# Block sums copied by transfer instead of VectorE, and expert 0's second weight loaded in two halves

## The chip, the cores and the metric

One core of a Trainium2 chip. The metric is the device time of one execution in microseconds (us), taken over several executions; "span" is the part of it that the trace covers, from the first to the last recorded instruction. A second number of each run is the mean granted TensorE clock over the span (1.000 is full speed all the time). All runs here count as fast runs: on a single core no other core tells a disturbed run apart. The engines are TensorE (PE in the profile), VectorE (DVE), ScalarE (ACT), POOL, which here also issues the loads, and SP, which here issues transfers and nothing else. A "hole" is a stretch in which TensorE stands idle.

## The reference, cut to what matters

Attention over batch 4, 8 heads, 768 positions of width 64. Each query sees the keys within 16 positions and 24 summaries, one for each block of 32 positions (maximum of the keys, mean of the values). The result is fed to a mixture of 8 experts, each of two matrices (512x1024 and 1024x512), with routing weights balanced by eight normalising rounds.

```python
k_sum = k.reshape(B, H, nb, block, D).max(axis=3)      # block = 32
v_sum = v.reshape(B, H, nb, block, D).mean(axis=3)
# ... near scores within 16 positions and block scores, one softmax over both ...
v_all = np.concatenate([v, v_sum], axis=2)
out_attention = np.matmul(a, v_all)
# ...
for e in range(E):
    h = np.maximum(x @ w1[e], 0.0)
    out += P[:, e:e + 1] * (h @ w2[e])
```

## The kernel before

The 32 (batch, head) combinations are worked as 16 pairs, which the text numbers 0 to 15. The attention stage takes about the first 115 us; expert 0 is threaded into it, and experts 1 to 7 follow. The first matmuls with expert 0's second weight (w2) are called the first projection. In pairs 4 to 15 (`i >= PB`) the last matmul of the values stage multiplies one 128-row matrix `V_e` (`NE` = 2 buffers) for each chunk of 128 positions: rows 0 to 63 hold the block sums of the two heads (`vs` on TensorE; written by `block_out` on VectorE, the same for all six chunks), rows 64 to 127 the values just outside the chunk ("near values"; the four small transfers that bring them, on SP for i < 12 (`BY_DMA`), are the near copies).

```python
def block_sums(i):                       # TensorE, into a PSUM bank of the ring "a"
    ...
def block_out(i):                        # VectorE: scales the sums, frees that bank
    vs = at.pop(("vs", i))[0:64, :].rearrange("p (j d) -> p j d", j=2)
    dst = V_s[i][0:64, :] if i < PB else V_e[i % NE][0:64, 0, :]
    nc.vector.tensor_tensor(out=dst..., in0=vs, in1=own_n..., op=ALU.mult)
    if i >= PB:                          # PB = 4; the same sums for chunks 1 to 5
        ve = V_e[i % NE]                 # NE = 2 buffers
        nc.vector.tensor_copy(out=ve[0:64, 1:G, :],
                              in_=ve[0:64, 0:1, :].to_broadcast([64, G - 1, 2 * VD]))

def near_values(i):                      # four small transfers, on SP for i < 12
    ...
def key_max(i):                          # VectorE, needs the transposed keys kT
    nc.vector.tensor_reduce(out=ks[r][:, 0, 0:24], in_=kT[r]..., op=ALU.max)

def scores(i):                           # TensorE
    sg = at["sg", i, 0] = banks2("sg")
    if i >= WHOLE:                       # WHOLE = 12: the second half of the scores
        dst[1] = [bank("a", "sg1") for _ in range(2)]    # takes two banks of ring "a"
    ...
```

No order of instructions is written down by hand. The kernel holds a list scheduler ("the planner"): each piece of work is a unit with an engine, an estimated cost, dependencies, a priority and a `lag`, the delay until others can use its result. The planner simulates the engines and so fixes each engine's program order; on the chip every engine then works through its own list. The keys and queries of pairs 12 to 15 are transposed by a transfer (units `kT`); the planner gives it 1.7 us plus a lag of 2.0.

```python
U["vs", i] = add("PE", 0.4, lambda: block_sums(i), [U["v", i], U.get(("A", i - NE, 1)), ...], opens=[buf])
U["Vs", i] = add("DVE", 0.28 if i < PB else 0.7, lambda: block_out(i), [U["vs", i], sc], uses=[buf])
U["near", i] = add("SP" if i < BY_DMA else "POOL", 2.4 ..., lag=5.0 ...)
U["kT", i, z] = add("DMA", 1.7, None, [U["tr", i, z]], prio, lag=2.0)
# ...
load_pair(PB, "kqv")                     # pair 4's keys, queries, values
load("w2", lambda: load_w2(0), 0.85, 4.0)   # 1 MB
```

The softmax here doesn't subtract the row's maximum and nothing guards it: scores larger than these inputs give would overflow.

Of the kernel before, what the change touches and what calls it, by code (L numbers as in the profile page):

```python
# [10 lines left out]
BF16 = mybir.dt.bfloat16  # L11
F16 = mybir.dt.float16
# [116 lines left out]
def kernel(  # L129
# [64 lines left out]
    def load_w2(e):  # L194
        w2s[e] = wpool.tile([128, KF, DM], F16, tag="w2", name="w2")
        nc.gpsimd.dma_start(out=w2s[e][:], in_=moe_w2[e].rearrange("(fk p) d -> p fk d", p=128))
# [21 lines left out]
    NQ = 6  # L218
    NB = PB
    NE = 2  # L220
    NS = 1
    NA = 3
    stage = ExitStack()
    with tc.manual_schedule():
# [22 lines left out]
        V_e = [attn.tile([128, G, 2 * VD], BF16, name=f"Ve{i}") for i in range(NE)]  # L247
# [110 lines left out]
        def block_out(i):  # L358
            vs = at.pop(("vs", i))[0:64, :].rearrange("p (j d) -> p j d", j=2)
            dst = V_s[i][0:64, :] if i < PB else V_e[i % NE][0:64, 0, :]  # L360
            nc.vector.tensor_tensor(out=dst.rearrange("p (j x) -> p j x", j=2)[:, :, 0:D], in0=vs,
                                    in1=own_n[:].to_broadcast([64, 2, D]), op=ALU.mult)
            if i >= PB:
                ve = V_e[i % NE]
                nc.vector.tensor_copy(out=ve[0:64, 1:G, :],
                                      in_=ve[0:64, 0:1, :].to_broadcast([64, G - 1, 2 * VD]))


        def near_values(i):

            sv, ve = v_x[i % NQ], V_e[i % NE]
            eng = nc.sync if i < BY_DMA else nc.gpsimd
            for j in range(2):
                c0, q0 = VD * j, 64 + 32 * j
                eng.dma_start(out=ve[q0 + W:q0 + 2 * W, 1:G, c0:c0 + VD],
                              in_=sv[128 - W:128, j, 0:G - 1, :])
                eng.dma_start(out=ve[q0:q0 + W, 0:G - 1, c0:c0 + VD],
                              in_=sv[0:W, j, 1:G, :])
# [48 lines left out]
        def values(i, h):  # L427
            sv, ee, ve, em = v_x[i % NQ], E_e[i % NE], V_e[i % NE], at["em", i]
            av = at["av", i, h] = bank("a", "av")
            for cc in range(HG):  # L430
                c, o = HG * h + cc, cc * 2 * VD
                for j in range(2):
                    nc.tensor.matmul(av[:, o + j * VD:o + (j + 1) * VD],  # L433
                                     lhsT=em[:, j, c, :], rhs=sv[:, j, c, :],
                                     start=(cc == 0 and j == 0), stop=False,
                                     skip_group_check=True)
            for cc in range(HG):
                c, o = HG * h + cc, cc * 2 * VD
                nc.tensor.matmul(av[:, o:o + 2 * VD], lhsT=ee[:, c, :], rhs=ve[:, c, :],  # L439
                                 start=False, stop=True, skip_group_check=True)  # L440
# [419 lines left out]
        def load(key, fn, issue, us, deps=()):  # L860
            last[0] = add("POOL", issue, fn, [last[0], *deps])
            last[1] = add("DMA", us, None, [add("RING", 0, None, [last[0]], lag=1.4 if last[1] else 0.9), last[1]], 100.0)
            U[key] = add("LAND", 0, None, [last[1]], lag=0.9)

        def load_pair(i, parts="kqv"):
            old = i - NQ
            for c in parts:
                if c == "v":
                    load(("v", i), lambda: load_v(i), 1.05, 1.85 if i < PB else 1.6,
                         [U.get(("A", old, 1)), U.get(("near", old))])  # L870
                elif i < PB and c in "qr":
                    h = "qr".index(c)
                    load(("q", i, h), lambda h=h: load_qk(i, 1, h), 0.65, 0.65)
                else:
                    z = "kq".index(c)
                    load((c, i), lambda z=z: load_qk(i, z), 0.75 if i < PB else 1.65,
                         1.2 if i < PB else 1.4, [U.get(("tr", old, z)), U.get(("tr", old, 2))])

        def pair_start(i, prio):
# [18 lines left out]
            if i >= PB:  # L898
# [3 lines left out]
                             [U["v", i]] + ([U.get(("A", i - NE, 1)), U["vc", i % NE]] if i >= PB else []), prio + 0.01, opens=[buf])  # L902
            sc = add("DVE", 0.25, lambda: summary_constants(i), [], prio - 1.0) if 0 < i < PB else None
            U["Vs", i] = add("DVE", 0.28 if i < PB else 0.7, lambda: block_out(i), [U["vs", i], sc],
# [37 lines left out]
        def pair_whole(i, prio):  # L942
            U["near", i] = add("SP" if i < BY_DMA else "POOL", 2.4 if i < BY_DMA else 3.0, lambda: near_values(i),
                               [U["v", i], U.get(("A", i - NE, 1)), U["vc", i % NE]], prio, lag=5.0 if i < BY_DMA else 3.5)
# [25 lines left out]
            for h in range(2):  # L970
                buf = Buffer("a")
                U["A", i, h] = add("PE", 0.4, lambda h=h: values(i, h),
                                   [U["mk", i, h], U["ed", i], U["sx", i, h], U["Vs", i], U["near", i]],
# [14 lines left out]
        def expert0(t0, xs):  # L988
# [3 lines left out]
            w = [U["w1", n] for n in range(4)]  # L992
# [16 lines left out]
            for c in range(HG):  # L1009
                buf = Buffer("m")  # L1010
                p0 = add("PE", 0.88, lambda c=c: project0(key, c, 0), evac[0:4] + [U["w2"]],
                         pr + 0.1 + c * 0.02, opens=[buf])
                p1 = add("PE", 0.88, lambda c=c: project0(key, c, 1), evac[4:8] + [p0],
# [37 lines left out]
        load_pair(PB, "kqv")  # L1051
        load("w2", lambda: load_w2(0), 0.85, 4.0)
        for n in range(NE):
            U["vc", n] = last[0] = add("POOL", 1.2, lambda n=n: value_constants(n), [last[0]])
# [37 lines left out]
        def transposed():  # L1092
# [6 lines left out]
            ve = V_e[(NP - 1) % NE]  # L1099
# [4 lines left out]
        last[0] = add("POOL", 0.3, transposed, [last[0], U["near", NP - 1]] + [U["kT", NP - 1, z] for z in range(2)]  # L1104
# [212 lines left out]
```

## Time and profile before

| | kernel before |
|---|---|
| time, median of 3 runs | 668.64 us (668.12 to 669.35) |
| span and clock of the profiled run | 666.7 us, 1.000 |
| TensorE busy | 657.9 us, 5132 matmuls |
| last matmul starts | 661.89 us |
| waits of TensorE between 5 and 640 us | 1.3 (w2), 0.5 and 0.3 (first loads), 0.2 (w1) |

The table says where time could be won: 2.3 us of waits in the first 35 us. The copy that the change takes off VectorE is one row in the view of the tile's instructions (least, median, largest ns; first and last start):

```profile
L365 DVE COPY Ve<-Ve x12: 483/483/485, 34.2 to 108.4; 64x650 bf16<-64x650 bf16 x12
```

The transfers between 36 and 70 us, by kind of copy (size of one, us from issue to landing) and by queue (packets, MB, time that the packets took as a share of 16 engines' span: above 100% more than one packet is under way on each engine), and two stretches (columns as in the prediction: busy time of PE, PEld, DVE, ACT, POOL, then clock, DMA share, GB/s):

```profile
Ve<-vx SPq DMA_DIRECT2D x20, 10.2 KB, 5.3
q0 software_dynamic: 36580, 4.60, 234.9%
q1 hardware_dynamic: 2220, 0.29, 10.8%
...
88.00:92.40 4.40, 4.40 (x50) 2.97 (x48) 4.15 (x11) 2.16 (x6) 2.10 (x4) 1.00 1.63 154
92.40:95.80 3.40, 3.40 (x51) 2.11 (x50) 2.41 (x5) 2.67 (x7) 0.00 (x0) 1.00 0.15 32
```

Between 36 and 70 us loads (q0) are under way all the time, more than two packets on each engine (the time that the packets took is 234.9% of 16 engines' span: above 100% more than one packet is under way on each engine), and a near copy takes 5.3 us from issue to landing.

### The profile page before, as it was taken

To read this page: it belongs to the slowest core of one execution; us is meant where nothing else is said; L and a number is where in the kernel's file an instruction comes from. 1 tells how busy PE (TensorE), PEld (TensorE's weight loads), DVE (VectorE), ACT (ScalarE), POOL (GpSimd) and SP (SyncE) were. 2 spreads that over 40 slices of the span, in tenths; PEclk is the share of its full clock that TensorE was granted. 3 is DMA by queue.
4 is the path that set the end of the run, shared out by engine and by line. 5 is a ranking of instruction groups with operands and counts; after the bars stand their busy time and mean duration, and the time that the engine had idled before them with its cause. 6 is when DMAs were issued, how large, how long until landed. Compare 5 with 4: busy or idle time off the path is not lost.

```text
span 666.7 us, 13260 instructions
## 1 busy us (share of the span) xinstructions
PE 657.9 (99%) x5132; PEld 434.0 (65%) x5132; DVE 549.2 (82%) x1035; ACT 410.5 (62%) x768; POOL 198.3 (30%) x256
## 2 busy tenths in 40 slices
PE   8999999999999999999999999999999999999996
PEld 4656665555676666666666666666666666666665
DVE  7889978799989787888789887888778877988776
ACT  6767766555986566556565665656665656556652
POOL 8899622100132222222221222222122213222123
PEclk9999999999999999999999999999999999999999
DMA  9999992700863647473654656373837465334656
GB/s 168 165 149 145 132 88 43 127 0 1 137 112 64 117 75 116 79 127 64 98 102 76 123 83 106 65 127 61 130 64 130 77 95 95 64 64 112 159 134 198
DMA packets 112542, 67.89 MB, mean 102 GB/s; under 512 B 77920, under 2 KB 90464, under 8 KB 112480
## 3 DMA queue, kind: packets, MB, share of 16 engines
q0 software_dynamic: 94800, 57.46, 65.7%
q1 hardware_dynamic: 17152, 9.58, 6.5%
q8 instruction: 40, 0.66, 0.4%
q14 instruction: 22, 0.18, 0.1%
q10 hardware_dynamic: 528, 0.02, 0.0%
HBM read 52.45 MB, written 6.29 MB: 88 GB/s over the span
## 4 chain that ended last, share of the span: by engine, by line
PE 94%; DMA 3%; POOL 2%; issue 0%; DVE 0%; ACT 0%; POOLq 0%; DVEq 0%
PE yps L813 22%; PE pA L762 22%; PE pY L813 17%; PE pQ L762 11%; PE yps L214 6%; PE hps L209 6%; PE pR L762 5%; DMA w<-in_moe_w_dram 3%; PE sg L345 1%; PE tkq L301 1%; PE av L433 1%; PE vs L355 1%; PE av L439 1%; POOL vx L287 1%; PE tx L548 1%; PE ss L459 1%
## 5 line engine op out<-in xcount | busy, mean ns | idle before, releaser
L813 PEld LDWEIGHTS <-h 128*128 128x128 f16 x2352 | 230.1, 98 | 89.3 <-issue 1.0
L841 POOL DMA_DIRECT2D out_acc<-y x120 | 101.5, 880 | 372.0 <-ACT y L837 97.8
L837 ACT ACTIVATE y<-pY,P_sb 128x256 f32<-128x256 f32 x168 | 79.8, 476 | 124.2 <-PE pY L813 122.5
L828 DVE SCALAR_TENSOR_TENSOR out_acc<-yps,P_sb,out_acc 128x512 f32<-128x512 f32 x128 | 95.2, 744 | 30.2 <-PE yps L813 30.0
L796 DVE TENSOR_TENSOR h<-h 128x1024 f16<-128x1024 f16 x168 | 109.0, 684 | 1.2
L813 PE MATMUL pY<-w,h 128*128 128x256 f16 x672 | 100.2, 273 | 0.6 <-ACT y L837 0.6
L762 PE MATMUL pA<-xT,w 128*128 128x512 f16 x336 | 98.5, 379 | 0.0
L813 PE MATMUL yps<-w2sum,h 128*128 128x256 f16 x672 | 98.1, 273 | 0.0
L813 PE MATMUL yps<-w,h 128*128 128x256 f16 x672 | 93.3, 273 | 0.0
L828 DVE SCALAR_TENSOR_TENSOR out_acc<-pY,P_sb,out_acc 128x512 f32<-128x512 f32 x84 | 62.9, 748 | 29.9 <-PE pY L813 28.2
L762 PEld LDWEIGHTS <-w 128*128 128x128 f16 x672 | 65.8, 98 | 30.9 <-issue 0.2
L762 PEld LDWEIGHTS <-w1sum 128*128 128x128 f16 x504 | 49.3, 98 | 44.2
L784 DVE CUSTOM_DVE_ANT_0 h<-pQ,snap 128x512 f16<-128x512 f32 x84 | 57.6, 685 | 6.0 <-ACT snap L205 3.3
L784 DVE CUSTOM_DVE_ANT_0 h<-pA,snap 128x512 f16<-128x512 f32 x84 | 57.3, 683 | 6.0 <-PE pA L762 5.9
L200 ACT ACTIVATE h<-pA 128x512 f16<-128x512 f32 x84 | 50.6, 603 | 12.4 <-PE pA L762 12.2
L200 ACT ACTIVATE h<-pR 128x512 f16<-128x512 f32 x84 | 50.1, 596 | 7.5 <-PE pR L762 7.4
L205 ACT COPY pR<-pA 128x512 f32<-128x512 f32 x84 | 48.0, 571 | 7.4 <-PE pA L762 6.4
L813 PE MATMUL pY<-w2sum,h 128*128 128x256 f16 x336 | 50.4, 273 | 0.0
L762 PE MATMUL pA<-xsum,w 128*128 128x512 f16 x168 | 50.0, 379 | 0.0
L762 PE MATMUL pQ<-xsum,w1sum 128*128 128x512 f16 x168 | 50.0, 379 | 0.0
L762 PE MATMUL pQ<-xT,w1sum 128*128 128x512 f16 x168 | 50.0, 379 | 0.0
L762 PE MATMUL pA<-xsum,w1sum 128*128 128x512 f16 x168 | 50.0, 379 | 0.0
(149 smaller groups left out, 845.9 us busy)
## 6 DMA issues: line engine op xcount, KB each, us to landing
out_acc<-y POOLq DMA_DIRECT2D x120, 256.0 KB, 3.4
w<-in_moe_w_dram POOLq DMA_DIRECT2D x15, 1024.0 KB, 10.6
out_dram<-out_acc SPq DMA_DIRECT2D x24, 256.0 KB, 2.5
qst<-in_q_dram POOLq DMA_DIRECT2D x32, 96.0 KB, 5.8
vx<-in_v_dram POOLq DMA_DIRECT2D x15, 192.0 KB, 6.6
kst<-in_k_dram POOLq DMA_DIRECT2D x24, 96.0 KB, 6.0
w<-in_moe_w_dram POOLq DMA_DIRECT2D x4, 256.0 KB, 7.9
kst<-in_k_dram POOLq DMA_DIRECT2D x3, 192.0 KB, 4.7
```

What stands on the lines that cost most here:

```text
L200: nc.scalar.activation(out=out, in_=in_, func=AF.Relu, bias=0.0, scale=1.0)
L205: (nc.scalar.copy if eng == "ACT" else nc.vector.tensor_copy)(out=out, in_=in_)
L209: nc.tensor.matmul(hp[:, 0:n], lhsT=w1s[e][:, dk, f * 128:(f + 1) * 128], rhs=xT[:, dk, t0:t0 + n], start=(dk == 0), stop=(dk == KD - 1))
L214: nc.tensor.matmul(yp[:, d], lhsT=h[:, f, c * 128:(c + 1) * 128], rhs=w2s[e][:, f, d], start=(f == 0), stop=(f == KF - 1))
L287: nc.gpsimd.dma_start(out=v_x[i % NQ][:].rearrange("p j g x -> p (j g) x")[:, :, 0:D], in_=v[b, h0:h0 + 2].rearrange("j (g p) d -> p (j g) ...
L762: nc.tensor.matmul(dst[:], lhsT=lhsT, rhs=rhs, start=first and k == 0, stop=k == HK - 1, skip_group_check=True)
L784: nc.vector._custom_dve(dve_ops.TENSOR_ADD_SAT, out=ring(e, p, q)[:, q % 2, blk, :], in0=at[src, e, p, q][:], in1=at.pop(("snap", n, e, p, ...
L796: nc.vector.tensor_tensor(out=h[:, :, out_, :], in0=h[:, :, a, :], in1=h[:, :, b, :], op=op)
L813: nc.tensor.matmul(dst[:, d], lhsT=lhsT, rhs=rhs, start=f == 0 and n in (1, 5, 2), stop=f == HF - 1, skip_group_check=True)
L828: nc.vector.scalar_tensor_tensor(out=o, in0=y, scalar=scalar, in1=o, op0=ALU.mult, op1=ALU.add)
L837: nc.scalar.activation(out=at[key][:, d], in_=src, func=AF.Copy, bias=0.0, scale=P_sb[:, t, e:e + 1])
L841: nc.gpsimd.dma_start(out=o, in_=at.pop(("y", e, p, c, key))[:], accum_op=ALU.add)
```

## The change

Its intent: free VectorE from twelve copies by letting a transfer spread the sums, with a third value buffer so that its latency can hide; take the wait for w2 away by letting half of it go ahead of pair 4's values; and give the planner the later landings that traces had shown.

```diff
-    def load_w2(e):
-        w2s[e] = wpool.tile([128, KF, DM], F16, tag="w2", name="w2")
-        nc.gpsimd.dma_start(out=w2s[e][:], in_=moe_w2[e].rearrange(...))
+    def load_w2(e, part=0, parts=1):
+        ...
+        fk = slice(part * KF // parts, (part + 1) * KF // parts)
+        nc.gpsimd.dma_start(out=w2s[e][:, fk, :], in_=moe_w2[e].rearrange(...)[:, fk, :])
+    NV = 3
-        V_e = [attn.tile([128, G, 2 * VD], BF16, name=f"Ve{i}") for i in range(NE)]
+        V_e = [attn.tile([128, G, 2 * VD], BF16, name=f"Ve{i}") for i in range(NV)]
-            if i >= PB:
-                ve = V_e[i % NE]
-                nc.vector.tensor_copy(out=ve[0:64, 1:G, :],
-                                      in_=ve[0:64, 0:1, :].to_broadcast([64, G - 1, 2 * VD]))
+        def spread_sums(i):
+            ve = V_e[i % NV]
+            (nc.sync if i < BY_DMA else nc.gpsimd).dma_start(
+                out=ve[0:64, 1:G, :], in_=ve[0:64, 0:1, :].to_broadcast([64, G - 1, 2 * VD]))
     # planner: landing lag of loads 0.9 -> 1.8 (k, q) and 2.3 (v, w2 halves) from pair 4 on
-            U["Vs", i] = add("DVE", 0.28 if i < PB else 0.7, lambda: block_out(i), ...)
+            U["Vs", i] = add("DVE", 0.28, lambda: block_out(i), ...)
+            U["sp", i] = add("SP" if i < BY_DMA else "POOL", 0.62 if i < BY_DMA else 0.9,
+                             lambda: spread_sums(i), [U["Vs", i]], prio, lag=5.0 if i < BY_DMA else 3.5)
-        load_pair(PB, "kqv")
-        load("w2", lambda: load_w2(0), 0.85, 4.0)
+        load_pair(PB, "kq")
+        load(("w2", 0), lambda: load_w2(0, 0, 2), 0.85, 2.0, (), 2.3)
+        load_pair(PB, "v")
+        load(("w2", 1), lambda: load_w2(0, 1, 2), 0.85, 2.0, (), 2.3)
     # (cut: NE -> NV wherever V_e is indexed; memsets of three buffers instead of two)
```

More of the change, by code (lines that the diff above doesn't have):

```diff
@@ L192, in load_w1 @@
             in_=moe_w1[e].rearrange("(dk p) f -> p dk f", p=128)[:, :, part * fw:(part + 1) * fw])
-    def load_w2(e):
-        w2s[e] = wpool.tile([128, KF, DM], F16, tag="w2", name="w2")
-        nc.gpsimd.dma_start(out=w2s[e][:], in_=moe_w2[e].rearrange("(fk p) d -> p fk d", p=128))
+    def load_w2(e, part=0, parts=1):
+        if part == 0:
+            w2s[e] = wpool.tile([128, KF, DM], F16, tag="w2", name="w2")
+        fk = slice(part * KF // parts, (part + 1) * KF // parts)
+        nc.gpsimd.dma_start(out=w2s[e][:, fk, :], in_=moe_w2[e].rearrange("(fk p) d -> p fk d", p=128)[:, fk, :])
     def relu(eng, out, in_):
@@ L359, in block_out @@
             vs = at.pop(("vs", i))[0:64, :].rearrange("p (j d) -> p j d", j=2)
-            dst = V_s[i][0:64, :] if i < PB else V_e[i % NE][0:64, 0, :]
+            dst = V_s[i][0:64, :] if i < PB else V_e[i % NV][0:64, 0, :]
             nc.vector.tensor_tensor(out=dst.rearrange("p (j x) -> p j x", j=2)[:, :, 0:D], in0=vs,
                                     in1=own_n[:].to_broadcast([64, 2, D]), op=ALU.mult)
-            if i >= PB:
-                ve = V_e[i % NE]
-                nc.vector.tensor_copy(out=ve[0:64, 1:G, :],
-                                      in_=ve[0:64, 0:1, :].to_broadcast([64, G - 1, 2 * VD]))
+        def spread_sums(i):
+            ve = V_e[i % NV]
+            (nc.sync if i < BY_DMA else nc.gpsimd).dma_start(
+                out=ve[0:64, 1:G, :], in_=ve[0:64, 0:1, :].to_broadcast([64, G - 1, 2 * VD]))
         def near_values(i):
-            sv, ve = v_x[i % NQ], V_e[i % NE]
+            sv, ve = v_x[i % NQ], V_e[i % NV]
             eng = nc.sync if i < BY_DMA else nc.gpsimd
@@ L427, in values @@
         def values(i, h):
-            sv, ee, ve, em = v_x[i % NQ], E_e[i % NE], V_e[i % NE], at["em", i]
+            sv, ee, ve, em = v_x[i % NQ], E_e[i % NE], V_e[i % NV], at["em", i]
             av = at["av", i, h] = bank("a", "av")
@@ L858, with load @@
         last = [None, None]
-        def load(key, fn, issue, us, deps=()):
+        def load(key, fn, issue, us, deps=(), lag=0.9):
             last[0] = add("POOL", issue, fn, [last[0], *deps])
             last[1] = add("DMA", us, None, [add("RING", 0, None, [last[0]], lag=1.4 if last[1] else 0.9), last[1]], 100.0)
-            U[key] = add("LAND", 0, None, [last[1]], lag=0.9)
+            U[key] = add("LAND", 0, None, [last[1]], lag=lag)
         def load_pair(i, parts="kqv"):
@@ L869, in load_pair @@
                     load(("v", i), lambda: load_v(i), 1.05, 1.85 if i < PB else 1.6,
-                         [U.get(("A", old, 1)), U.get(("near", old))])
+                         [U.get(("A", old, 1)), U.get(("near", old))], 0.9 if i < PB else 2.3)
                 elif i < PB and c in "qr":
@@ L876, in load_pair @@
                     load((c, i), lambda z=z: load_qk(i, z), 0.75 if i < PB else 1.65,
-                         1.2 if i < PB else 1.4, [U.get(("tr", old, z)), U.get(("tr", old, 2))])
+                         1.2 if i < PB else 1.4, [U.get(("tr", old, z)), U.get(("tr", old, 2))], 0.9 if i < PB else 1.8)
         def pair_start(i, prio):
@@ L901, in pair_start @@
             U["vs", i] = add("PE", 0.4, lambda: block_sums(i),
-                             [U["v", i]] + ([U.get(("A", i - NE, 1)), U["vc", i % NE]] if i >= PB else []), prio + 0.01, opens=[buf])
+                             [U["v", i]] + ([U.get(("A", i - NV, 1)), U["vc", i % NV]] if i >= PB else []), prio + 0.01, opens=[buf])
             sc = add("DVE", 0.25, lambda: summary_constants(i), [], prio - 1.0) if 0 < i < PB else None
-            U["Vs", i] = add("DVE", 0.28 if i < PB else 0.7, lambda: block_out(i), [U["vs", i], sc],
+            U["Vs", i] = add("DVE", 0.28, lambda: block_out(i), [U["vs", i], sc],
                              prio + 0.01, uses=[buf])
@@ L943, in pair_whole @@
             U["near", i] = add("SP" if i < BY_DMA else "POOL", 2.4 if i < BY_DMA else 3.0, lambda: near_values(i),
-                               [U["v", i], U.get(("A", i - NE, 1)), U["vc", i % NE]], prio, lag=5.0 if i < BY_DMA else 3.5)
+                               [U["v", i], U.get(("A", i - NV, 1)), U["vc", i % NV]], prio, lag=5.0 if i < BY_DMA else 3.5)
+            U["sp", i] = add("SP" if i < BY_DMA else "POOL", 0.62 if i < BY_DMA else 0.9, lambda: spread_sums(i), [U["Vs", i]],
+                             prio, lag=5.0 if i < BY_DMA else 3.5)
             x1 = []
@@ L972, in pair_whole @@
                 U["A", i, h] = add("PE", 0.4, lambda h=h: values(i, h),
-                                   [U["mk", i, h], U["ed", i], U["sx", i, h], U["Vs", i], U["near", i]],
+                                   [U["mk", i, h], U["ed", i], U["sx", i, h], U["sp", i], U["near", i]],
                                    prio, opens=[buf])
@@ L991, in expert0 @@
             pr = 1000.0 + n
-            w = [U["w1", n] for n in range(4)]
+            w, w2_0 = [U["w1", n] for n in range(4)], [U["w2", n] for n in range(2)]
             evac, old = [], [U.get(("pj", halves[n - 2], c)) for c in range(HG)] if n >= 2 else []
@@ L1010, in expert0 @@
                 buf = Buffer("m")
-                p0 = add("PE", 0.88, lambda c=c: project0(key, c, 0), evac[0:4] + [U["w2"]],
+                p0 = add("PE", 0.88, lambda c=c: project0(key, c, 0), evac[0:4] + [w2_0[0]],
                          pr + 0.1 + c * 0.02, opens=[buf])
-                p1 = add("PE", 0.88, lambda c=c: project0(key, c, 1), evac[4:8] + [p0],
+                p1 = add("PE", 0.88, lambda c=c: project0(key, c, 1), evac[4:8] + [p0, w2_0[1]],
                          pr + 0.11 + c * 0.02, uses=[buf])
@@ L1050 @@
                     load_pair(i, "r")
-        load_pair(PB, "kqv")
-        load("w2", lambda: load_w2(0), 0.85, 4.0)
+        load_pair(PB, "kq")
+        load(("w2", 0), lambda: load_w2(0, 0, 2), 0.85, 2.0, (), 2.3)
+        load_pair(PB, "v")
+        load(("w2", 1), lambda: load_w2(0, 1, 2), 0.85, 2.0, (), 2.3)
+        for n in range(NV):
+            U["vc", n] = last[0] = add("POOL", 1.2, lambda n=n: value_constants(n), [last[0]])
         for n in range(NE):
-            U["vc", n] = last[0] = add("POOL", 1.2, lambda n=n: value_constants(n), [last[0]])
             U["ec", n] = last[0] = add("POOL", 0.7, lambda n=n: edge_constants(n), [last[0]])
@@ L1098, in transposed @@
                 nc.gpsimd.tensor_copy(out=warm[:, 4:5], in_=xT[0:32, PB - 2, (B - 1) * S:(B - 1) * S + 1])
-            ve = V_e[(NP - 1) % NE]
+            ve = V_e[(NP - 1) % NV]
             for j in range(2):
@@ L1102, in transposed @@
                                       in_=ve[64 + 32 * j:96 + 32 * j, G - 2, VD * j:VD * j + 1])
-        last[0] = add("POOL", 0.3, transposed, [last[0], U["near", NP - 1]] + [U["kT", NP - 1, z] for z in range(2)]
+        last[0] = add("POOL", 0.3, transposed, [last[0], U["near", NP - 1], U["sp", NP - 1]] + [U["kT", NP - 1, z] for z in range(2)]
                       + [U["x", i] for i in range(X_BY_DMA, NP - 1)])
```

## The prediction

> **What bounds the kernel now.** I read the page's busy table first, then the waits of TensorE over the whole run, the stretches, the chain that ended last around its one hole, and last the transfer queues.
>
> ```profile
> PE 657.9 (99%) x5132; PEld 434.0 (65%) x5132; DVE 549.2 (82%) x1035; ACT 410.5 (62%) x768; POOL 198.3 (30%) x256
> PE 94%; DMA 3%; POOL 2%; issue 0%; DVE 0%; ACT 0%; POOLq 0%; DVEq 0%
> ```
>
> TensorE is busy 657.9 of 666.7 us and makes up 94% of the chain. The next answer lists its waits in the first 200 us, the one after cuts the run into stretches (columns: busy time of PE, PEld, DVE, ACT, POOL; clock; DMA share, where 1 would be all 16 engines always holding one packet; GB/s).
>
> ```profile
> PE yps L214 <- DMA w<-in_moe_w_dram: 1.3, 1, 1.3
> ...
> 30.00:36.00 6.00, 4.66 (x73) 3.08 (x71) 4.92 (x14) 3.40 (x6) 5.90 (x8) 1.00 1.72 170
> 36.00:40.00 4.00, 4.00 (x42) 2.23 (x41) 3.01 (x10) 2.41 (x4) 3.60 (x6) 1.00 2.42 150
> 40.00:60.00 20.00, 20.00 (x259) 13.15 (x258) 18.74 (x48) 14.25 (x23) 19.85 (x24) 1.00 2.46 146
> ```
>
> From 36 us on TensorE has no hole: asked for its waits between 36 and 640 us, the trace lists none. DVE is nearly full (18.74 of 20) and POOL too, but neither is waited for. So only TensorE's holes can be won, and the one this change aims at is here:
>
> ```profile
> 24.24 10.49 DMA w<-in_moe_w_dram
> 34.73 0.04 issue
> 34.77 1.02 PE yps L214 x4
> ```
>
> Expert 0's w2 (1 MB) is issued at 24.24 and lands at 34.73; the first projection starts 0.04 later, after 1.34 us idle. The other holes (start-up, and the last evictions and stores after the last matmul at 661.9) are not touched.
>
> **What the Trainium skill says.** "Perfetto Trace Analysis", Identifying the Most-Contended Engine: matmul busy share is a poor measure of headroom, as matmuls are pipelined. The trace agrees (a 512-column matmul lasts 379 ns, yet eight take 1.89 us), so I also summed the spacing of matmul starts against their columns at 2.4 columns per ns, the rate the spacing itself shows: between 40 and 640 us only 0.1 to 0.4 us in ten is over, so no hidden reserve is there. "DMA: Bandwidth & Descriptors", Queues, rings and completion order: each transfer engine takes turns between queue rows, a packet at a time. The trace agrees: the small Ve copies take 5.0 to 5.6 us to land while loads run (32 to 60 us), and 1.7 to 2.8 when hardly anything runs (100 to 110 us). The same page, Anatomy of one DMA: semaphore waits happen on the issuing sequencer before dispatch. So on SP a copy that waits holds up those behind it; here SP issues pair 5's first copy at 39.41, right after its v landed at 39.33.
>
> **The change part by part.**
>
> 1. *w2 in two loads around v of pair 4.* Pair 4's q lands at 26.89, its v at 29.04 (2.15 us more), w2 at 34.73 (5.69 us for 1 MB). The queue is in order, so by shares: first half 26.89 + 2.85 = 29.7, v 31.9, second half 34.7. In the built order the first projection stands earlier than before. Adding up the groups ahead of it with their spacings from the trace (four-matmul hidden groups 0.70, value groups 0.80 and so on), it comes at 31.6, its second half at 36.9, and pair 4's block sums at 34.4. All three find their data. **Gain: 1.34 us plus about 0.15 of pipeline drain, 1.5 us.**
>
> 2. *Spread by DMA.* Twelve DVE copies of 64x650 at 483 ns (5.8 us) go. DVE is not waited for by TensorE, so this is worth nothing directly. In their place come 12 transfers of 64 partitions x 5 runs of 260 bytes, 83 KB. Values of a pair now wait for vs -> block_out -> transfer, where a 0.48 us copy stood.
>
> 3. *Third value buffer.* One more set of POOL memsets: 0.74+0.20+0.09+0.09, with gaps 1.33 us. Together with the second w2 issue (0.9), the loads of pair 5 and later are issued about 2.1 us later (29.2 -> 31.3). They need not land 2.1 later: these loads take about 6 us from issue while q and k of pair 4 took 4.5 to 4.8, so some 1.5 us of it is queueing that shrinks. I take landings 0.1 to 0.6 later. In return a pair's near copies may start before the pair two earlier is done.
>
> 4. *Planner constants.* TensorE's work is the same (5132 matmuls), in another order: values of pairs 4 to 15 come on average some 4 us earlier (pair 15 at about 110 against 115), for which the schedule gives up slack it had.
>
> **Where the gain can go again.** The queues in two windows of 4 us, 36.5 to 40.5 without near copies and 41.5 to 45.5 with them (packets, MB, share):
>
> ```profile
> q0 software_dynamic: 4806, 0.60, 242.8%
> ...
> q0 software_dynamic: 3980, 0.50, 231.9%
> q1 hardware_dynamic: 378, 0.04, 11.3%
> ```
>
> 378 small packets displaced 826 packets of the loads: 2.2 each. So the queues are full, and a spread of 320 packets takes some 700 places at 1,200 per us, 0.6 us per pair; landings now come every 4.35 us and would slip by up to that per pair. A spread has 20 packets per engine where one near copy has 5, so I estimate its landing at 6.0 to 6.6 us from issue, against 5.4 of a near copy. Now the deadlines, with TensorE's times added up as above:
> - Pair 4: block sums at 34.4, spread issued at about 35.7, lands 41.7 to 42.3; values at 41.7. Late by 0 to 0.6.
> - Pair 5: v at 39.4 to 39.9, four near copies of 0.63, the spread at 42.0 to 42.5, lands 48.0 to 49.1; values at 47.1. Late by 0.9 to 2.0.
> - Pair 7: its spread stands behind the near copies of pair 8 on SP, which wait for v of pair 8 (52.15 before; 52.4 to 54 with slip). Spread at 55 to 56.6, lands 61 to 63; values at 60.0. Late by 1 to 3.
> Lateness counts from the same undisturbed order, so it is not added: the largest one is what TensorE loses, as it has no other work in a fixed order. From pair 8 on the slack is 4 us and more. **Loss: 0.3 to 3 us, middle 1.6.** Sum: -1.5 + 1.6, about zero.
>
> **The rivals.** (a) *The wait on w2 simply goes* and every spread lands in time: 667.1. For it: the planner's landing constants were raised to what traces show, and TensorE's start times before agree with its order within 0.3 us; against: it leaves a spread only the latency of a near copy. (b) *The spread becomes the wait* of the values groups at pairs 4 to 7, as worked out: 668 to 670. For it: full queues, no slack. (c) *DVE relief pays*: 5.8 us at a DVE 94% busy. Against: no PE wait on DVE after 36 us; worth 0, so 667 at best, as in (a). (d) *Loads slip as a whole*, each pair by 0.6 us over eight pairs, and block sums of pairs 13 and 14 or the transposes wait for loads: 671 or more. Against: without slip v of pair 13 would land at 75.0 and is needed at 78.7, of pair 14 at 82.7 and 86.6, so 3.8 us of room plus whatever TensorE has lost by then.
>
> **Range and chances.** From 668.64: best case -1.5 (667.1), middle +0.1, bad case -1.5 + 3.5 (670.6); repeats of the kernel before spread by 0.6 each way. I predict 668.7 us, 667.1 to 670.7 in 8 of 10. A change of 2% is 13.4 us, nine times the hole to be won and four times the worst lateness: chances 0.005 faster, 0.985 within, 0.01 slower.
>
> **What would show it.** Right on part 1: no wait of yps on w in the waits of TensorE, first projection at about 31.6. Right on (b): new TensorE waits at the values groups (av<-Ve,Ee) released by a DMA of Ve, between 41 and 62 us, of 0.3 to 3 us in all, and spreads landing over 5.6 us after issue. Load landings per pair further apart than 4.35 us would show the slip. The prediction is wrong if spreads land as quickly as near copies (then (a), 667), if waits on k, q or v loads appear (d), or if the first projection still waits for its half of w2.

## The result, and the profile after

| | before | changed |
|---|---|---|
| time, median of 6 runs each | 668.38 us (666.76 to 669.35) | 670.32 us (667.30 to 671.36) |
| span and clock of the profiled run | 666.7, 1.000 | 669.0, 0.997 |
| last matmul starts | 661.89 | 664.06 |
| last matmul to the end of the span | 4.81 | 4.94 |
| time minus span | 1.7 | 2.3 to 2.4 |

The ratio is 1.0025, with a 95% interval of 1.0002 to 1.0048: the same within 2%, and on the slow side of equal. (Ratios in this document are the mean time of one kernel's fast runs over that of the other's in the same rounds, so they are not quite the ratio of the medians.) The page's busy table and its clock row, then all waits of TensorE between 36 and 640 us (us in total, times, longest):

```profile
PE 660.2 (99%) x5132; PEld 435.6 (65%) x5132; DVE 544.9 (81%) x1022; ACT 412.1 (62%) x769; POOL 202.7 (30%) x265
PEclk9999989999999999999999999999999999999999
...
PE sg L348 <- DVE Ve L364: 1.5, 1, 1.5
PE av L444 <- DMA Ve<-Ve: 0.5, 1, 0.5
```

The wait on w2 is gone: the halves landed at 28.26 and 32.73 us and the first projection did not wait. VectorE is 4.3 us less busy, and nothing came of it. Two new holes are there where the kernel before had none.

**The smaller hole** is the predicted one. The timeline of SP shows the last near copy of pair 8, which had waited for pair 8's values (they landed at 52.18), and behind it the spreads of pairs 7 and 8 (x2), as the new transfer of the block sums is called; then TensorE (start, duration, and in brackets the idle time before and what ended it):

```profile
54.14 0.60 SPq L382 DMA_DIRECT2D Ve<-vx  x1
54.84 1.72 SPq L371 DMA_DIRECT2D Ve<-Ve  x2
...
60.91 0.28 PE L444 MATMUL av<-Ve,Ee 128*128 128x130 bf16 x2 [0.54 <-DMA Ve<-Ve]
```

The spread of pair 7 was issued at 54.84 and landed 6.0 us later.

**The larger hole** is not in the prediction's sum; its rival (d) had named transposes that wait for late loads, and had set them aside. TensorE and VectorE around 90 us, the transfer at the head of the chain, and last the same scores in the kernel before:

```profile
89.98 0.45 PE L348 MATMUL sg<-qT,kT 64*128 64x160 bf16 x7
91.88 0.36 PE L348 MATMUL sg<-qT,kT 64*128 64x160 bf16 x5 [1.46 <-DVE Ve L364]
...
90.68 0.95 DVE L336 TENSOR_REDUCE ks<-kT 128x24 bf16<-128x768 bf16 x1 [2.68 <-DMA kT<-kst]
91.55 0.28 DVE L364 TENSOR_TENSOR Ve<-vs,own_n 64x128 bf16<-64x128 f32 x1
...
81.96 8.70 DMA kT<-kst
...
94.44 0.59 PE L345 MATMUL sg<-qT,kT 64*128 64x160 bf16 x12
```

L348 are the scores of pair 12, whose second half needs two banks of PSUM ring "a". One of them still held the block sums of pair 14, which L364 (`block_out`) empties. The sums were ready, but in VectorE's program L336 (`key_max` of pair 14) stands ahead of L364, and VectorE stood 2.68 us until the transposed keys of pair 14 had landed. "PSUM — Partial Sum Buffer", Engine vs sequencer instructions, in the Trainium skill says that VectorE's queue is strictly first in, first out; the trace agrees, as a ready instruction waited behind one that was not. The chain of waits goes back from the scores over L364 and the key maximum to the transfer itself, issued at 81.96 and landed 8.70 later; the planner had counted on 3.7. In the kernel before these keys landed at 88.92 and no wait followed: there the scores of pair 12 start at 94.44. The new plan had moved them 4.5 us forward, to 89.98, while the keys landed 1.7 us later.

**After that hole the clock fell.** Two stretches, the one with the hole and the one behind it:

```profile
88.00:92.40 4.40, 2.94 (x48) 1.79 (x46) 1.28 (x4) 2.98 (x7) 1.06 (x2) 0.99 2.17 140
92.40:95.80 3.40, 3.40 (x12) 1.66 (x11) 1.02 (x2) 0.90 (x2) 2.24 (x5) 0.52 0.86 113
```

Twelve matmuls in a stretch where the kernel before did 51 (many of them smaller), TensorE busy all the time, at a clock of 0.52: the clock record shows half speed from 92.27 us for 3.41 us, and the 384-column matmuls follow each other every 320 ns in place of 160. Half of 3.41, so 1.7 us, is lost.

So the profiled execution adds up: 0.54 and 1.46 us of new holes and 1.7 us of slow clock are 3.7; waits of 1.3, 0.5, 0.3 and 0.2 us less are 2.3. The difference, 1.4, is less than the 2.2 us by which the last matmul is later; some 0.8 us are missing. Most of them lie in the small waits, which are gone from the list but hardly from the time: the same eight matmuls of the hidden layer start at 23.69 us here and at 23.93 in the kernel before, so 0.24 us are won ahead of the wait on w2 and not the 1.0 of the list. Another 0.13 us lies between the last matmul and the end of the span, and 0.6 outside the span.

The queues between 36 and 70 us:

```profile
Ve<-Ve SPq DMA_DIRECT2D x7, 81.2 KB, 6.0
q0 software_dynamic: 34323, 4.32, 200.0%
q1 hardware_dynamic: 4357, 0.76, 19.9%
```

2137 more small packets came with 2257 fewer packets of the loads. The values of pairs 5 to 12 landed 4.71 us apart on average, against 4.31 before.

**How typical is this execution?** It was the slowest of its six runs. A half-clock stretch of 3.41 us takes 0.0026 off the mean clock of the span, so the five other runs, with clocks of 0.998 to 1.000, had none, and four of them (669.58 to 670.40 us) were slow all the same. The slow clock explains the profiled run's extra, not the median. Those runs have no trace, so what their holes were is not known.

### The profile page after: what moved, and what is told of

Its sections match the earlier page's. It is cut to its first block, busy times and chain, and to the rows that moved or that the text cites. A ratio compares the mean times of both kernels' runs of the same rounds, so it can differ in the third digit from the quotient of the medians.

```text
span 669.0 us, 13278 instructions
## 1 busy us (share of the span) xinstructions
PE 660.2 (99%) x5132; PEld 435.6 (65%) x5132; DVE 544.9 (81%) x1022; ACT 412.1 (62%) x769; POOL 202.7 (30%) x265
## 3 DMA queue, kind: packets, MB, share of 16 engines
HBM read 52.45 MB, written 6.29 MB: 88 GB/s over the span
## 4 chain that ended last, share of the span: by engine, by line
PE 94%; DMA 3%; DVE 2%; issue 0%; ACT 0%; SPq 0%; DVEq 0%
PE yps L818 22%; PE pA L767 22%; PE pY L818 16%; PE pQ L767 11%; PE hps L211 6%; PE pR L767 5%; PE yps L216 5%; DMA kT<-kst 1%; PE sg L348 1%; DMA Ve<-Ve 1%; DMA kvf<-in_v_dram 1%; PE tkq L304 1%; PE av L515 1%; PE vs L358 1%; PE av L438 1%; PE av L444 1%
## 5 line engine op out<-in xcount | busy, mean ns | idle before, releaser
L833 DVE SCALAR_TENSOR_TENSOR out_acc<-yps,P_sb,out_acc 128x512 f32<-128x512 f32 x128 | 95.3, 745 | 29.3 <-PE yps L818 29.2
L202 ACT ACTIVATE h<-pA 128x512 f16<-128x512 f32 x84 | 50.6, 603 | 12.3 <-PE pA L767 12.2
L207 ACT COPY pR<-pA 128x512 f32<-128x512 f32 x80 | 45.6, 570 | 8.5 <-PE pA L767 7.6
L211 PE MATMUL hps<-xT,w 128*128 128x384 f16 x256 | 50.5, 335 | 0.0
L767 PE MATMUL pR<-xT,w 128*128 128x512 f16 x168 | 50.0, 379 | 0.0
```

Of the source, the lines that this page charges most:

```text
L202: nc.scalar.activation(out=out, in_=in_, func=AF.Relu, bias=0.0, scale=1.0)
L207: (nc.scalar.copy if eng == "ACT" else nc.vector.tensor_copy)(out=out, in_=in_)
L211: nc.tensor.matmul(hp[:, 0:n], lhsT=w1s[e][:, dk, f * 128:(f + 1) * 128], rhs=xT[:, dk, t0:t0 + n], start=(dk == 0), stop=(dk == KD - 1))
L767: nc.tensor.matmul(dst[:], lhsT=lhsT, rhs=rhs, start=first and k == 0, stop=k == HK - 1, skip_group_check=True)
L833: nc.vector.scalar_tensor_tensor(out=o, in0=y, scalar=scalar, in1=o, op0=ALU.mult, op1=ALU.add)
```

## The experiments

All twelve runs gave correct results. Each batch ran on one chip with its own runs of the kernel before; their medians were 668.09, 667.03, 668.13 and 667.06 us, so only ratios within a batch are compared.

### 1. The changed kernel again

No edit.

> The changed kernel once more, for a second profile. Theory (two late transfers): TensorE waits again at the values of pair 7 for its spread (0.3 to 1.0 us), and again at the scores of pair 12 for about 1 to 2 us, because DVE stands in front of the key maxima of pair 14 until its transposed keys land and block_out behind it frees a PSUM bank late; a stretch at half clock of about 3.4 us follows. Rival (chance): the hole at the scores belongs to that one execution, and this profile has only the first wait and a time near 667.5.

Measured: 669.22 us (668.83 to 675.13), ratio 1.003 (0.999 to 1.0069). The profiled execution was again the slowest, with the same two holes, both larger (two waits of 0.6 us on first loads are left out):

```profile
PE sg L348 <- DVE Ve L364: 2.2, 1, 2.2
PE av L444 <- DMA Ve<-Ve: 1.9, 1, 1.9
```

The keys of pair 14 took 12.24 us to land here, from 82.22 to 94.46, although the load that they come from had landed at 77.23, before the 77.74 of the kernel before: here it was SP, busy until 82.04 with the transfer ahead, and the long transfer itself, and not a late load. Each hole was followed by 3.41 us at half clock (from 62.38 and from 96.51 us). The holes are a property of the kernel's plan; their size is one of the execution (in experiment 8 the larger one is absent).

### 2. The two loads of w2 alone

```diff
 # kernel before, with:
-        load_pair(PB, "kqv")
-        load("w2", lambda: load_w2(0), 0.85, 4.0)
+        load_pair(PB, "kq");  load(("w2", 0), ..., 2.0, (), 2.3)
+        load_pair(PB, "v");   load(("w2", 1), ..., 2.0, (), 2.3)
```

> The kernel before with only the two loads of w2 around v of pair 4. If the gain is real and was given back by the rest: no TensorE wait on w, 1.3 to 1.5 us faster than before (about 667.0). If splitting w2 only moves the wait (rival): a new wait on a load or on the second half, and 668 or more.

Measured: 668.14 us (666.98 to 670.26), ratio 0.9997 (0.9972 to 1.0022). No wait on w2 is left; the waits of TensorE between 5 and 640 us are

```profile
PE vs L357 <- DMA vx<-in_v_dram: 0.5, 1, 0.5
PE tkq L312 <- DMA qst<-in_q_dram: 0.5, 1, 0.5
```

The hole of 1.34 us is removed and the median does not move. The fastest run of the kernel before took 666.67 to 667.0 us in each of the four batches (spans of 664.9 to 665.3 us), and this kernel's fastest 666.98 (span 664.9): so it seems that the hole, seen in one execution, is not there or far smaller in many others. That is argued from times, as only one execution of the kernel before has a trace here. A rival is not excluded: in this kernel's own trace the last matmul starts at 661.50 us, only 0.4 earlier than in the trace of the kernel before, so most of the gain was given back there, the 0.5 us wait for a values load at 17.8 us being new.

### 3. Everything but the spread by transfer

```diff
 # changed kernel, with:
+            if i >= PB:
+                nc.vector.tensor_copy(out=ve[0:64, 1:G, :], in_=ve[0:64, 0:1, :].to_broadcast(...))
-            U["sp", i] = add("SP" ..., lambda: spread_sums(i), ...)
+            U["sp", i] = U["Vs", i]                 # and cost 0.7 for block_out again
```

> The changed kernel, but block sums are spread by the DVE copy as before (three buffers, split w2 and landing constants kept). If the spread transfers are the cause of the loss: no wait on Ve, loads land 0.3 to 0.6 us per pair earlier, 667 to 667.5. If late transposed keys are the cause whatever spreads: a hole of 1 us or more between 80 and 100 us stays, 668.5 to 670.5.

Measured: 667.89 us (667.67 to 668.66), ratio 0.9991 (0.9969 to 1.0013), clock 1.000. The waits:

```profile
PE tkq L313 <- DMA qst<-in_q_dram: 0.6, 1, 0.6
PE vs L358 <- DMA vx<-in_v_dram: 0.5, 1, 0.5
PE lp L570 <- DVE xT L207: 0.3, 1, 0.3
```

Neither new hole is there, and the values land 4.33 us apart as in the kernel before. Both holes and the slip of the loads therefore come with the spread by transfer, not with the third buffer, the two loads or the landing constants alone. The transfers and the plan made for them are not separated by this: without them the planner puts the scores of pair 12 at 94.23 us again, and not at 89.98. Against experiment 1 of the same batch, where no run is below 668.83, no run here is above 668.66.

### 4. Telling the planner how late transposed keys land

```diff
-                    U["kT", i, z] = add("DMA", 1.7, None, [U["tr", i, z]], prio, lag=2.0)
+                    U["kT", i, z] = add("DMA", 1.7, None, [U["tr", i, z]], prio, lag=6.0)
```

> The changed kernel with one planner constant altered: transposing transfers are taken to land 6.0 us after their 1.7 us instead of 2.0 (measured: 7.5 to 9.9 us from issue). If the keys of pair 14 are the main cause: the wait at the scores of pair 12 and the half-clock stretch go, the 0.5 us wait at pair 7 stays, 667.3 to 668.0. If full queues are the cause: the hole comes back at another place and the time stays at 669.5 or more.

Measured: 668.18 us (667.12 to 671.80), ratio 0.9997 (0.9973 to 1.0021). The hole at 90 us is gone: in the new order block sums of pair 14 come ahead of its key maximum (92.19 us, the keys landing at 93.58). In the profiled execution, once more the slowest, the spread of pair 7 landed 1.9 us late (0.5 was expected), and half clock for 3.41 us followed (smaller waits left out):

```profile
PE av L444 <- DMA Ve<-Ve: 1.9, 1, 1.9
```

The median is that of the kernel before, though the interval overlaps that of experiment 1. The one number also changes the order of all engines, so it does not yet show that VectorE's order was the cause. The next four kernels leave the planner's order as it is and move single instructions.

### 5. Only SP's order: spread 7 ahead of the near copies of pair 8

```diff
-        for u in plan.order():
+        order = plan.order()
+        order.remove(U["sp", 7]); order.insert(order.index(U["near", 8]), U["sp", 7])
+        for u in order:
```

> The changed kernel with one transfer moved on SP: the spread of pair 7 is issued ahead of the near copies of pair 8; every other engine's order is the same. If standing behind those copies made it late: issued by 53 us, landed by 59, no TensorE wait on Ve at pair 7; the hole at the scores of pair 12 stays. If full queues made it late (rival): it still lands over 7 us after issue and TensorE still waits 0.5 us or more.

Measured: 671.99 us (671.24 to 673.61), ratio 1.0073 (1.0052 to 1.0093). The spread was issued at 52.02 instead of 54.84 and landed at 57.61, in time. But:

```profile
PE sg L348 <- DVE Ve L364: 2.9, 1, 2.9
PE av L444 <- DMA Ve<-Ve: 0.2, 1, 0.2
```

The hole at 90 us is twice its size in the changed kernel's first trace, with 6.83 us at half clock from 92.17 us on; the clocks of 0.993 to 0.997 say that all four runs had such a stretch. TensorE came 0.35 us earlier to the scores of pair 12 (89.63 instead of 89.98), and the keys of pair 14 landed 1.04 later (91.70 instead of 90.66). The first is what a hole mended upstream does where a later transfer sets the time; whether the second comes of the move is not shown, as these keys landed at 94.46 in the repeat without it. In this trace the mended hole is given back later, and more than that.

### 6. Only VectorE's order: block sums of pair 14 ahead of its key maximum

```diff
+        order.remove(U["ks", 14]); order.insert(order.index(U["Vs", 14]) + 1, U["ks", 14])
```

> The changed kernel with one DVE instruction moved: the key maxima of pair 14 come right after block_out of pair 14 instead of right before. If DVE waiting there for the transposed keys holds the PSUM bank: no TensorE wait at the scores of pair 12, no half-clock stretch after it, 1.5 to 3.2 us off the trace; the wait for the spread of pair 7 stays. If the bank is late for another reason (rival): the hole stays above 1 us.

Measured: 669.63 us (669.0 to 670.14), ratio 1.0037 (1.0016 to 1.0058). The twelve score matmuls are now one piece, and no half clock follows:

```profile
89.98 0.59 PE L348 MATMUL sg<-qT,kT 64*128 64x160 bf16 x12
...
93.50 0.81 PE L211 MATMUL hps<-xT,w 128*128 128x384 f16 x4 [0.87 <-DVE h L204]
```

This shows the cause of the larger hole: one instruction moved on VectorE, and it is gone, with the trace 2.3 us shorter as expected. The median is no better than the changed kernel's in its two batches (ratios 1.0025 and 1.003), so this hole alone does not explain the median. The wait at pair 7, expected to stay, is absent here: waits of 0.6 and 0.4 us on first loads had delayed TensorE, and the spread landed at 60.84. It also shows what is behind the hole: VectorE still stands for the same keys (3.29 us, to 91.77) and now the hidden layer's evictions behind that wait are late, which costs TensorE 0.87 us.

### 7. Both moves

> Both moves. If the two waits (and the half clock after them) are the whole loss: no TensorE wait over 0.3 us between 36 and 640 us and 1.2 to 1.6 us faster than before, about 666.7 to 667.2. If a next wait takes their place (rival): 668 or more.

Measured: 668.56 us (667.51 to 670.74), ratio 1.0021 (1.0003 to 1.0039). The trace has a single wait:

```profile
PE vs L358 <- DMA vx<-in_v_dram: 0.4, 1, 0.4
```

Here the last matmul starts at 660.83 us, 1.06 earlier than in the trace of the kernel before, and yet the run took 668.10. What it loses again is at the end: 4.93 us from the last matmul to the end of the span, and 2.3 outside it. The time is as the rival had it, but without the next wait that it named. Why its other runs reach 670.74 is not to be seen in the one trace and stays open.

### 8. Filling the larger hole

```diff
+                if i == WHOLE and g == HG:
+                    keep_busy(*7 * [512])       # seven matmuls of zeros between the halves of the scores
```

> The changed kernel with seven matmuls of zeros (7 x 216 ns = 1.5 us) put between the two halves of the scores of pair 12, where the hole is; all else in the same order. If the half clock comes from TensorE standing idle for about 1.5 us or more: the clock record shows no half-clock stretch after 85 us, and the trace is 1.5 us or more shorter than the changed kernel's for the same lateness of the keys. If the half clock has another cause (rival): the stretch stays, and the trace is the same or longer.

Measured: 670.33 us (670.0 to 673.42), ratio 1.0055 (1.0031 to 1.0079). In the profiled execution the keys of pair 14 happened to land at 88.93, so there was no hole to fill, and the filler cost its 1.5 us. The wait at pair 7 was 1.2 us here and no half clock followed it. Inconclusive on what the filler does to the clock.

### 9. The later memsets

```diff
 # experiment 3, with:
-        for n in range(NV):
+        for n in (1, 2):
             U["vc", n] = last[0] = add("POOL", 1.2, lambda n=n: value_constants(n), [last[0]])
+            # the third buffer, first used by pair 6, after the loads of pair 5 are issued
```

> Block sums spread by the DVE copy, split w2, three value buffers, and the memsets of the buffer that pair 6 uses first issued on POOL after the loads of pair 5 instead of before them. If the 0.5 us waits on q and v loads come from the loads issued late behind the memsets: those waits shrink to under 0.3 us in all and the time is 1.0 to 1.5 us below before. If the loads land as late anyway, the queue being full (rival): the same waits, within 0.5 us of before.

Measured: 668.54 us (668.12 to 668.97), ratio 1.0004 (0.9989 to 1.0019). A miss: the values of pair 5 are issued at 33.52 instead of 33.71, those of pair 6 at 39.42 instead of 37.95 (experiment 3), and nothing is won; the waits stay, as the rival said.

### 10. Two value buffers, the copy on VectorE

```diff
 # experiment 3, with:
-    NV = 3
+    NV = 2
```

> Block sums spread by the DVE copy, split w2, but two value buffers, as before. If the third buffer is worth something: values of pairs wait for the near copies, TensorE waits on Ve appear or the time is 0.5 us or more above the three-buffer version (so 668.3 or more where before is 668). If it only costs POOL time (rival): 0.3 to 1.3 us below before.

Measured: 667.20 us (667.02 to 667.70), ratio 0.9987 (0.9973 to 1.0000). This is 0.9 us below the kernel before, as the rival said. It looked like the best version, so it ran once more as experiment 12.

### 11. The spread by transfer with a better plan

```diff
+                    U["kT", i, z] = add("DMA", 1.7, None, [U["tr", i, z]], prio, lag=6.0)
+            # near copies of pair i only after the spread of pair i - 1 is issued; memsets as in 9
```

> Block sums spread by DMA, with the planner told of both: each pair's spread is issued before the next pair's near copies, transposing transfers land 6.0 us after their 1.7 us; the third buffer's memsets come after the loads of pair 5. If late spreads and late transposed keys were the whole loss: no wait on Ve and none at the scores of pair 12, 0.5 to 1.5 us below before. If transfers on a full queue lose against the DVE copy whatever the order (rival): other waits on loads, 0.5 us or more above the two DVE versions.

Measured: 668.23 us (667.37 to 672.0), ratio 1.0009 (0.9988 to 1.0031). One wait of 0.5 us on a first load is left, and the last matmul starts at 660.21, the earliest of all traces here; 667.6 us all the same, because 5.23 us to the end of the span and 2.2 outside it follow. The spread can be planned in without a hole, and is still no faster than the kernel before. Neither text was right: no other wait took the place of the two, and nothing was won.

### 12. Experiment 10 again, five rounds

> The version with the copy on VectorE, w2 in two loads and two value buffers once more, in five rounds, because its interval against the kernel before touched 1.0. Theory (the wait on w2 gone at no new wait): median 667.0 to 667.4, ratio 0.9975 to 0.9990, every run between 666.9 and 667.9, and from the last matmul to the end of the recorded span 4.49 us again, with time minus span 1.8 us. Rival (the earlier gain was the scatter of the kernel before): ratio 0.9995 to 1.0005 with runs as spread as those of the kernel before.

Measured: 667.14 us (667.02 to 669.10) against 667.06 (666.78 to 668.37) of the kernel before, ratio 0.9997 (0.9983 to 1.0011). The rival is right: no version is shown to beat the kernel before. This version's usual runs do scatter less (four within 0.22 us). Its slow one has a trace, and it shows a third place for the slow clock, in the first loads (two of its waits, then the stretch from 8 to 14 us):

```profile
PE tkq L313 <- DMA qst<-in_q_dram: 0.8, 1, 0.8
PE vs L358 <- DVE vx L207: 0.5, 1, 0.5
...
8.00:14.00 6.00, 5.54 (x79) 3.40 (x80) 4.48 (x9) 3.12 (x6) 6.00 (x9) 0.72 1.85 162
```

Waits of 0.2, 0.8 and 0.5 us lie close together ahead of 3.41 us at half clock from 8.29 us, and the run took 2.0 us longer than its neighbours. The trace of the same kernel in experiment 10 has only 0.54 and 0.22 us there, and no half clock. Runs of the kernel before at 671 us with a clock of 0.994 to 0.997, three in the first batch, may have the same reason; they have no trace, so this is not shown.

## Why the prediction was right or wrong

The time was predicted at 668.7 us, and 667.1 to 670.7 holds the median of 670.32. The mechanism of the loss that it named, the late spread at pair 7, is there, but two of its steps failed (5 and 6 below), and a part that it left out (7) counts. That the median lies within the range is therefore partly luck: terms were missing on the side of the loss, and the profiled run itself (671.36 us) lies outside.

1. **w2 in two loads: right in its wait, too generous in its gain.** The wait is gone and the halves came earlier than worked out (28.3 and 32.7 us). The "gain: 1.5 us" was read off one execution of the kernel before; done alone, the part gave a ratio of 0.9997, where 1.5 us would be 0.9977, though its interval (0.9972 to 1.0022) does not quite exclude that.
2. **VectorE relief worth nothing: right.** 4.3 us less busy, and after 36 us there was no wait of TensorE on it to remove; the only one afterwards is new.
3. **Late spread at pair 7 (rival b): right.** Issue at 55 to 56.6, landing at 61 to 63, late by 1 to 3 us, said the text; 54.84, 60.87 and 0.54 us are the trace's, and 56.44, 62.39 and 1.9 in the repeat. Pairs 4 and 5, said to be late by up to 0.6 and 2.0, were in time: their spreads took 4.3 and 4.9 us to land, where "6.0 to 6.6" had been estimated for all; 6.2 is the median of those up to 80 us.
4. **Loads slip: right in kind, smaller in size.** 0.4 us a pair instead of up to 0.6. Between 36 and 70 us one small packet more stood against about one packet of the loads less (2137 against 2257), where 2.2 had been taken over from the near copies. "So the queues are full" was read too strongly: in the kernel before POOL was busy issuing (19.85 of 20 us), the values of pairs 5 to 10 were issued 4.37 us apart on average, and each values load took 6.2 to 6.9 us, so the landings came at the pace of the issue. Only with the spreads did the loads fall behind: issued 4.25 us apart, they took from 5.2 us (pair 5) up to 7.8 (pair 11). The longer landings of near copies under load, which the text gave for transfer engines taking turns, fit this but do not show the turns: the quick ones at 100 to 110 us were issued by POOL, not by SP. The loads of pair 5 were issued at 29.82, where "29.2 -> 31.3" stood: the delay was 0.6 us, as the loads ahead of them were issued sooner (pair 4's queries at 20.24 instead of 21.62).
5. **"From pair 8 on the slack is 4 us and more": the step that failed.** It measured slack only for the values that the spread feeds. The new plan also brought the scores of pair 12 forward (94.44 to 89.98 us), and VectorE's program had an instruction on the transposed keys of pair 14 ahead of one that these scores needed; the keys landed 8.70 us after issue (12.24 in the repeat). The largest hole of the kernel came from there, 1.46 and 2.23 us. A slip of the loads had part in it in the first trace, where the transfer was issued at 81.96, right after its load had landed at 81.82 (77.74 in the kernel before), but not in the repeat. Rival (d) came near, but its room of 3.8 us was again that of values. It could have been read before the run: the built program's order of VectorE shows the key maximum of pair 14 ahead of its block sums, and the trace of the kernel before has a median of 7.8 us for such transfers, against 3.7 in the planner.
6. **"Lateness is not added: the largest one is what TensorE loses": half right, one term missing.** Experiment 6 shows that repairing one hole uncovers another, and 0.35 us of the growth in experiment 5 fit it. But a hole can also have a price after it, which the sum did not have: 1.7 us of slow clock in the profiled run, and some 3.0 in experiment 5 (half of 6.83, less the part that was idle).
7. **The ends of the program were said not to be touched.** From the last matmul to the end of the run the traced execution of the kernel before needs 6.6 us, like experiment 2; every kernel with the spread by transfer 7.1 to 7.4; experiments 3, 9, 10 and 12 6.3 to 6.5. About 0.7 of the 1.9 us between the medians is therefore not in the attention stage at all. Between experiments 1 and 3, which differ in the spread alone, it is 1.0 (7.27 against 6.29) of the 1.3 us between the medians. In the traces the part of it within the span is a longer end of the POOL engine's final drain (4.15 us after the last matmul instead of 4.03, and 3.70 in experiments 2, 3 and 10). Why it and the time outside the span differ from kernel to kernel stays open.

## What to carry to other kernels

Here a copy moved from an engine that nobody waited for into busy queues bought nothing. In the plan as it stood it cost its own latency, the slip of the loads, and a hole where an engine's fixed order stood behind a late transfer; with a better plan (experiment 11) the holes went and still nothing was won. Before believing in slack, look in the built order of every engine for an instruction that stands ahead of a needed one and waits for a transfer. And a hole seen in one trace is worth its length only if the median of the runs has it too; do the part alone before counting on it.

## What the Trainium skill lacked or had wrong

- "TensorE: Matmul & The Clock Gate", Why this matters for your kernels, asks for no idle gaps over about 3 us. Here single gaps of 1.46, 1.91, 1.94, 2.23 and 2.86 us were followed by half clock, and so were three of 0.22, 0.79 and 0.50 close together; gaps of 0.87 (experiment 6), 1.2 (experiment 8) and 1.34 us (kernel before) were not. The page's section A second HAM failure mode does tell of a clock that falls through frequent short idles, but without a length. What its Part 1 says of the windows agrees: each half-clock stretch inside the run lasted 3.41 or 6.83 us, and the full-clock stretches before or between them were multiples of that (30.72 us in experiment 1 is 9 times 3.413, 85.33 in the changed kernel's trace 25 times). Idle time in such a window does not settle it alone: at the end of the program windows with 1.83 (experiment 3) and 1.94 us idle (kernel before) were not followed by half clock, while one with 1.46 inside the run was.
- "DMA: Bandwidth & Descriptors", Anatomy of one DMA, gives 2.0 us plus size over 436 KB per us, which makes an estimate of 2.2 us for 96 KB. Near copies of 10 KB took 1.7 to 2.8 us when little else ran, which fits; beside other transfers 96 KB loads took a median of 5.6 to 6.2 us (36 to 70 us, both kernels), spreads of 81 KB inside SBUF 4.3 to 8.2, and the transposed keys of pairs 12 to 14 7.0 to 12.2. No page gives the landing time of a transfer beside others, which is what a plan needs.
- "Runtime: NRT & Kernel Launch" lists the stages after a kernel with one time for each; that the time at the end can differ from kernel to kernel is on no page: 6.3 to 7.4 us from the last matmul to the end of the run here, though the work after the last matmul is the same.
